# Sliding-block attention layers scored in 64x64 blocks, and unread matmuls also in the banks of a unit's tail

## The chip, the cores and the metric

The kernel runs on one core of one Trainium2 chip. A core has a matrix engine (TensorE, PE in the profile, with its weight loads as PEld), a vector engine (VectorE, DVE), a scalar engine that does the exps (ScalarE, ACT), a general engine (GpSimd, POOL) that here sets constants and issues some transfers, and a queue engine (SyncE, SP) that issues the others. Matmuls write to PSUM, eight banks of 512 fp32 columns in each of 128 partitions. The metric is the device time of one execution in microseconds.

## The reference, cut to what matters

Four layers alternate between kind A, a sliding-block attention, and kind B, a full one. Both have 2048 positions, 640 features, and 32 heads of 20.

```python
def attention(x, wqkv, wo, windowed):
    qkv = (x @ wqkv).reshape(B, S, 3, H, Dh).transpose(2, 0, 3, 1, 4)
    q, k, v = qkv[0], qkv[1], qkv[2]
    scores = jnp.einsum("bhqd,bhkd->bhqk", q, k) * (Dh ** -0.5)
    if windowed:                       # kind A, W = 256
        idx = jnp.arange(S)
        mask = (idx[:, None] - idx[None, :] >= 0) & (idx[:, None] - idx[None, :] < W)
        scores = jnp.where(mask[None, None], scores, -1e9)
    p = softmax(scores)
    o = jnp.einsum("bhqk,bhkd->bhqd", p, v)
    return o.transpose(0, 2, 1, 3).reshape(B, S, D) @ wo

x = x + attention(layernorm(x), A_wqkv, A_wo, True)
x = x + attention(layernorm(x), B_wqkv, B_wo, False)
x = x + attention(layernorm(x), A_wqkv, A_wo, True)
x = x + attention(layernorm(x), B_wqkv, B_wo, False)
```

In kind A a position sees itself and the 255 before it, so three 128-wide blocks of keys at most meet a 128-wide block of queries, and two of these three are cut by a diagonal.

## The kernel before

**Units and banks.** The work of attention is cut into units: one layer, one chunk of 512 queries (c, four of them) and one group of four heads (g, eight of them). The heads of a group lie in four strips of 32 partitions, so that a score matmul uses 32 rows of PE and four heads use four different strips. Scores are transposed: keys lie on the 128 PSUM partitions, queries on the columns. A *bank* is one PSUM bank of scores of one head. A full layer has 16 banks a head and unit, one for each block of 128 keys. A sliding-block layer has three banks a head and unit (`window_banks`): the six blocks of keys that a chunk of 512 queries can see are packed two into a bank, each over the query blocks that see it, so that a bank's 512 columns are filled: 128 + 384, 256 + 256 and 384 + 128. That is 1536 columns a head and chunk; the first chunk has only 512, 384 and 256. Each of these banks is multiplied after its exp by one of three patterns of zeros and ones (`masks`).

**Tiles and the main loop.** The banks of all units stand in one list, which is cut into *tiles* of three banks (in the early stretch three and two in turn). One turn of the main loop, a tick, does this for one tile: the score matmuls (L1222) into PSUM banks 0 to 2 or 3 to 5, in two rounds, first the first block of each bank and then the second; the exps (L1253), one ACT instruction for each run of banks with the same first column, into the tile `pt`; then other work that is let in by a credit (`pump`); then the value matmuls (L1289) of a group of four heads whose exps lie two or three ticks back, into bank 7; then the masking of the tile before (L1325, DVE). The order in which the instructions are written is the order in which they run on each engine.

**The other work.** Projections (`project`, L353, and `t_v`, L444), output projections (`t_out`, L530), layer norms (`t_ln`) and the *tail* of each unit (`t_tail`: column sums, their reciprocal, its spreading over the strips, and the product, in steps with waits of two ticks between them) are generators in a list `todo`, sorted by when they are needed. They take the PSUM banks that the tiles leave free, through `take_m` and `drop_m`: bank 6, and in the early stretch bank 5 too. `evac` copies a result out of PSUM, on ACT before the first unit of layer 1 and on DVE afterwards (`state["act"]`). Results for later layers are staged in `st` (pool `stp`, four tiles) and written to DRAM by POOL.

**The unread matmuls.** A clock is granted to PE at full or at half rate. `keep_clock` (L613) counts the PE work of a tick in `state["heat"]`, in units of one 512-column matmul, and while that is less than one for each bank (less a `surplus` carried over from the tick before), first lets in other work and then writes matmuls of the identity whose results nobody reads, into a free bank; if no bank is free it returns. It acts from the first unit of layer 1 (`woven`) to the end of layer 3's first chunk. In the tail of the very last unit `fill` (L981) does the same.

**The order of units.** Layer 0's units come first; layer 1's first chunk is mixed in as soon as its keys are there. Layer 2's units are mixed into layer 1's chunks 1 to 3 and the first chunk of layer 3. The rest of layer 3 stands alone.

## Time and profile before

| | |
|---|---|
| median of 4 runs | 2369.64 us (2365.09 to 2378.36) |
| the profiled execution's own time | 2370.41 us |
| its span, first to last instruction | 2368.7 us |
| mean granted clock of PE | 0.809 |
| exps of 1536 columns (L1253) | 1366, mean 1560 ns |
| exps of 1024 columns | 194, mean 1075 ns |
| unread matmuls (L613) | 549, 195.2 us busy |
| masks (L1325) | 403, 239.2 us busy |
| casts of projections to `st` on ACT (L302) / DVE (L304) | 23 / 127 |

By shape, the scores of the sliding-block layers are 512 matmuls of 384 columns (84.1 us busy), 448 of 256 (50.5 us) and 448 of 128 (53.0 us); their value matmuls are 512 of 384 (46.8 us), 448 of 256 (26.2 us) and 448 of 128 (28.1 us).

How to read the profile: it is one execution, its engines side by side. "Busy" is the time in which an engine runs at least one instruction, "idle before" the time it stood still in front of the instructions of a group, with what ended the wait. The chain is followed back from the last instruction to whatever released each step. Matmuls overlap, so the mean length of one says little of how many run in a microsecond; the distances of their starts do.

### The profile page before, as it was taken

The numbers are of one execution on the slowest core, as the hardware profiler recorded it, in microseconds if no ns is written. First come the engines' busy times: TensorE is split into PE (matmuls) and PEld (weight loads), VectorE is DVE, ScalarE is ACT, GpSimd is POOL, SyncE is SP. The second block draws the span as 40 slices with busy tenths as digits, with TensorE's granted clock in tenths as the row PEclk, the third lists the DMA queues.
The fourth block names the chain that finished last, engine by engine and source line by source line (L and its number), as shares of the span: only waits on it lengthen the run. The fifth ranks groups of instructions, "written<-read, shape, count | busy, mean of one in ns | idle before, by whom it ended". The sixth has DMA issues, their size and how long they took to land.

```text
span 2368.7 us, 40024 instructions
## 1 busy us (share of the span) xinstructions
PE 2030.5 (86%) x15554; PEld 708.9 (30%) x15554; DVE 1458.8 (62%) x2724; ACT 2184.9 (92%) x1753; POOL 142.9 (6%) x295
## 2 busy tenths in 40 slices
PE   8888999878888888888888888888878888888887
PEld 3433333323322332223322333232322222222222
DVE  7677775426646666656666544352577777777772
ACT  7778889898999998999899999999999999999997
POOL 3111110100000001000010011001000000000000
PEclk9999999997988998979997999889655565556556
DMA  6232422322300223102331034022111010001100
GB/s 183 72 96 80 109 64 58 83 62 64 82 19 27 57 68 93 37 14 54 75 93 32 3 86 118 29 42 73 51 34 37 26 38 26 26 26 38 38 14 12
DMA packets 173678, 132.53 MB, mean 56 GB/s; under 512 B 115760, under 2 KB 156080, under 8 KB 173488
## 3 DMA queue, kind: packets, MB, share of 16 engines
q1 hardware_dynamic: 163872, 101.39, 17.3%
q0 software_dynamic: 9616, 28.59, 3.5%
q8 instruction: 122, 2.00, 0.4%
q14 instruction: 68, 0.56, 0.1%
HBM read 98.70 MB, written 27.79 MB: 53 GB/s over the span
## 4 chain that ended last, share of the span: by engine, by line
ACT 36%; PE 31%; issue 16%; DVE 13%; DMA 2%; SPq 1%; POOL 0%; ACTq 0%; DVEq 0%; POOLq 0%
ACT pt L1253 35%; PE ps L1222 8%; PE ps L353 6%; PE ps L1289 5%; PE ps L530 4%; DVE pt L1325 3%; PE ps L444 3%; PE ps L613 2%; DMA wqk<-in_B_wqkv_dram 1%; DVE on L1020 1%; DVE st L304 1%; ACT ka L1253 1%; DVE oT L810 1%; DVE raw_o L858 1%; PE ps L1016 1%
## 5 line engine op out<-in xcount | busy, mean ns | idle before, releaser
L1253 ACT ACTIVATE pt<-ps 128x1536 bf16<-128x1536 f32 (+2 forms) x1641 | 2107.2, 1461 | 139.4 <-PE ps L1222 127.5
L1222 PE MATMUL ps<-qt,kt 32*128 32x512 bf16 x4008 | 671.2, 477 | 204.0 <-ACT pt L1253 173.4
L1289 PE MATMUL ps<-pt,vt 128*21 128x512 bf16 x3860 | 488.3, 478 | 1.0 <-DVE raw_o L796 0.7
L1222 PEld LDWEIGHTS <-kt 32*128 32x128 bf16 x4008 | 190.8, 94 | 650.8 <-issue 631.1
L1325 DVE TENSOR_TENSOR pt<-pt,masks 128x1024 bf16<-128x1024 bf16 (+5 forms) x403 | 239.2, 627 | 134.8 <-ACT pt L1253 134.2
L353 PE MATMUL ps<-xnT,wqk 128*128 128x512 bf16 x830 | 225.5, 397 | 25.5 <-DMA wqk<-in_B_wqkv_dram 10.8
L1289 PEld LDWEIGHTS <-vt 128*21 128x21 bf16 x3960 | 100.6, 91 | 335.6 <-issue 328.1
L613 PE MATMUL ps<-masks,ident 128*128 128x512 bf16 x549 | 195.2, 430 | 5.4 <-DVE rT L1008 2.0
L304 DVE CAST st<-ps 128x512 bf16<-128x512 f32 x127 | 87.8, 691 | 168.8 <-PE ps L353 168.3
L530 PE MATMUL ps<-wop,on 128*128 128x320 bf16 x976 | 170.7, 319 | 7.5 <-DVE on L1020 3.3
L1222 PE MATMUL ps<-qa,ka 32*128 32x384 bf16 (+2 forms) x1408 | 118.5, 278 | 35.6 <-ACT pt L1253 29.3
L858 DVE TENSOR_SCALAR xnT<-ps 128x512 int32<-128x512 f32 x88 | 60.8, 691 | 106.8 <-PE ps L851 104.2
L1020 DVE TENSOR_TENSOR on<-oT,ps 128x512 bf16<-128x512 bf16 x128 | 87.4, 683 | 60.9 <-PE ps L1016 60.5
L810 DVE CAST oT<-ps 128x512 bf16<-128x512 f32 x112 | 76.8, 686 | 72.4 <-PE ps L1289 46.7
L539 DVE TENSOR_TENSOR x_sb<-x_sb,ps 128x320 bf16<-128x320 bf16 x120 | 57.9, 482 | 101.7 <-PE ps L530 101.7
L444 PE MATMUL ps<-wv,xnT 128*128 128x320 bf16 x640 | 112.3, 309 | 7.5 <-DVE va L304 1.5
L530 PEld LDWEIGHTS <-on 128*128 128x128 bf16 x976 | 91.4, 102 | 75.4 <-issue 40.0
L353 PEld LDWEIGHTS <-wqk 128*128 128x128 bf16 x830 | 72.5, 99 | 125.9 <-issue 54.9
L1289 PE MATMUL ps<-pt,va 128*21 128x384 bf16 (+2 forms) x1408 | 80.4, 291 | 3.0 <-DVE pt L1325 1.8
L1222 PEld LDWEIGHTS <-ka 32*128 32x128 bf16 x1408 | 44.6, 92 | 104.9 <-issue 95.6
L444 PEld LDWEIGHTS <-xnT 128*128 128x128 bf16 x640 | 56.7, 99 | 50.4 <-issue 31.2
L1016 PE MATMUL ps<-rT,spread 32*128 32x128 bf16 x512 | 60.7, 250 | 5.3 <-DVE vs L304 2.1
(105 smaller groups left out, 1590.7 us busy)
## 6 DMA issues: line engine op xcount, KB each, us to landing
vt<-v_d SPq DMA_DIRECT2D x48, 336.0 KB
kt<-k_d SPq DMA_DIRECT2D x192, 80.0 KB
wqk<-in_B_wqkv_dram SPq DMA_DIRECT2D x80, 160.0 KB
wqk<-in_A_wqkv_dram SPq DMA_DIRECT2D x70, 160.0 KB
k_d<-st POOLq DMA_DIRECT2D x75, 128.0 KB, 2.2
q_d<-st POOLq DMA_DIRECT2D x75, 128.0 KB, 2.1
qt<-q_d SPq DMA_DIRECT2D x384, 20.0 KB
v_d<-vs POOLq DMA_DIRECT2D x16, 336.0 KB, 3.6
```

What stands on the lines that cost most here:

```text
L304: nc.vector.tensor_copy(out=out_, in_=in_)
L353: nc.tensor.matmul(pq, lhsT=wt[:, dc, :], rhs=xt[:, dc, :], start=(dc == 0), stop=(dc == KD - 1),)
L444: nc.tensor.matmul(pv, lhsT=xt[:, dc, i * P : (i + 1) * P], rhs=wv_sb[l % 2][:, dc, h * HD : (h + 1) * HD], start=(dc == 0), stop=(dc == K ...
L530: nc.tensor.matmul(yp, lhsT=on[:, g, qb * P : (qb + 1) * P], rhs=wop[:, g, i * HD : (i + 1) * HD], start=(g == g0), stop=(g == G - 1),)
L613: nc.tensor.matmul(ps[:, b, :], lhsT=ident[:], rhs=masks[:, 0, :], start=True, stop=True)
L810: nc.vector.tensor_copy(out=oT[:], in_=op)
L858: V.tensor_scalar(out=xi.bitcast(I32)[:, i * C : (i + 1) * C], in0=side["psum"], scalar1=SCALE * LOG2E * E23, scalar2=127.0 * E23, op0=ALU ...
L1020: nc.vector.tensor_tensor(out=on[:, g, :], in0=oT[:], in1=zb, op=ALU.mult)
L1222: nc.tensor.matmul(sp[:, i, col * P : (col + qn) * P], lhsT=u.k(kc, j), rhs=u.q(j, q0, qn), start=True, stop=True,)
L1253: nc.scalar.activation(out=pt[:, i:k, b0 * P :], in_=sp[:, i:k, b0 * P :], func=ACT.Exp, scale=SCALE,)
L1289: nc.tensor.matmul(op[32 * j : 32 * j + VW, q0 * P : (q0 + qn) * P], lhsT=u.v(kc, j), rhs=pg[:, i, col * P : (col + qn) * P], start=(first ...
L1325: nc.vector.tensor_tensor(out=pt_[:, i:k, b0 * P :], in0=pt_[:, i:k, b0 * P :], in1=mv_, op=ALU.mult,)
```

## The change

**Sliding-block scores.** The keys of a chunk are cut into blocks of 64 instead of 128. A score matmul has 64 keys (`half` 0 or 1 of a 128-wide block) as weights and writes the lower or the upper 64 PSUM partitions, over just those 64-wide query blocks that see its keys. A head and unit still has three banks: two *masked* windows of 512 columns (448 in the first chunk), each with three low and three high matmuls, and one bank of *pairs* of 256 columns (128 in the first chunk) that needs no mask. In all that is 1280 columns a head and chunk, 1024 in the first. The score loop now writes, for each bank of a tile, a low and a high matmul, and goes round until the longest list is done. If a tile holds any sliding-block bank, its full banks are scored in halves too.

**Exps.** A run of banks with the same first and last column is one instruction; before, only the first column counted, and it reached to the bank's end.

**Masks and values.** In two of a window's eight 64-wide columns the low and the high partitions hold different blocks of keys for different queries. The high half of these is multiplied into a separate small tile `phi` (a new pool of four), and the two stretches of three columns that hold diagonals and these high halves are multiplied in place, by `tri`, four 64-wide patterns in place of `masks`. The value matmuls read `phi` for those columns and `pt` for the others. `stp` has three tiles instead of four.

**Unread matmuls.** `keep_clock` keeps a `carry` of up to 3 over the ticks; the heat of the scores is no longer added; the least heat is the tile's width in columns/512, divided by 3, times 1.76 (times 1.0 in front of `woven`, where nothing was asked for until now). A tail that takes a bank writes an unread matmul into it first (`warm_bank`) when the heat is below the least and no other work can be let in. The unread matmul reads the identity four times over instead of `masks`. In a tile of sliding-block banks the credit for other work is scaled by its width/2.5.

By the order of instructions, the number of exps goes from 1641 to 1699, the masks from 403 to 524 instructions, the score matmuls of the sliding-block layers from 1408 to 3712, their value matmuls from 1408 to 2752, the unread matmuls from 558 to 658, and the casts to `st` on ACT from 23 to 14. POOL and SP issue the same transfers as before.

```diff
+B = 64
+    phip = pool("phip", 4)
-    stp = pool("stp", 4)
+    stp = pool("stp", 3)
-    masks = big.tile([P, 3, C], BF16, name="masks", tag="masks")
+    tri = big.tile([P, 4, B], BF16, name="tri", tag="tri")
+    idents = ident[:].unsqueeze(1).to_broadcast((P, 4, P))
...
+    def cool():
+        return state["heat"] + state["carry"] < state["least"]
+    def unread(b):
+        nc.tensor.matmul(
+            ps[:, b, :].rearrange("p (a b) -> p a b", a=4), lhsT=ident[:], rhs=idents,
+            start=True, stop=True,
+        )
+        state["heat"] += 1.0
+    def warm_bank(b):
+        if cool() and (
+            state["credit"] <= 0.0 or all(task.wake > state["tick"] for task in todo)
+        ):
+            unread(b)
-    def keep_clock(least):
-        while state["heat"] < least:
+    def keep_clock():
+        while cool():
             t = choose(False)
             if t is not None and state["credit"] > -0.5:
                 state["credit"] -= advance(t)
                 continue
             b = min(mfree, key=mfree.get)
             if mfree[b][0] > state["tick"]:
-                return
+                break
+            unread(b)
+        spare = state["heat"] + state["carry"] - state["least"]
+        state["carry"] = min(max(spare, 0.0), 3.0)
+        state["heat"] = 0.0
...
+    def windows(c):
+        found = []
+        for o in range(2):
+            k, q = 4 * c + o, 2 * o
+            low = [(k, q, 5, 1), (k + 2, q + 4, 2, 6)]
+            high = [(k, q + 1, 5, 2), (k + 2, q + 5, 1, 7)]
+            values = [
+                (k, q, 5, 1, False), (k + 2, q + 4, 2, 6, False), (k, q + 5, 1, 6, True),
             ]
+            if c > 0:
+                low.append((k - 2, q, 1, 0))
+                high.insert(1, (k - 2, q, 2, 0))
+                values = [(k - 2, q, 1, 0, False), *values, (k - 2, q + 1, 1, 1, True)]
+            else:
+                high[0] = (k, q, 6, 1)
+            found.append(((0 if c > 0 else B, C), True, low, high, values))
+        pairs = [(4 * c + 2, 6, 2, 0)] + [(4 * c - 1, 0, 2, 2)] * (c > 0)
+        found.append(((0, 2 * B * len(pairs)), False, pairs, pairs, [(*p, False) for p in pairs]))
...
         mb = yield from take_m()
+        warm_bank(mb)
         zp = ps[:, mb, 0:16]
...
+        def mask(pt, hi, i, k, first):
+            v = pt[:, i:k, :]
...
+            nc.vector.tensor_tensor(
+                out=hi["t"][:, i:k, int(first) :, :], in0=w[:, :, 6 if first else 1 : 7 : 5, :],
+                in1=tri[:, 3:4, :].unsqueeze(1).to_broadcast((P, n, 2 - first, B)), op=ALU.mult,
+            )
...
+            x = bass.AP(v.tensor, v.offset, [(ps_, pn), (ss, n), (5 * B, 2), (1, 3 * B)])
+            m = tri[:, 0:3, :].rearrange("p b e -> p (b e)")
+            nc.vector.tensor_tensor(
+                out=x, in0=x,
+                in1=m.unsqueeze(1).unsqueeze(1).to_broadcast((P, n, 2, 3 * B)), op=ALU.mult,
+            )
...
-                for n in range(2):
-                    for i, (u, j, m, b0, subs, first, last, end) in enumerate(cur):
-                        for kc, q0, qn, col in subs[n : n + 1]:
+                for n in range(0, max(len(x) for x in jobs), 2):
+                    for i, x in enumerate(jobs):
+                        for half, lhsT, rhs, col in x[n : n + 2]:
+                            rows = slice(0, P) if half is None else slice(B * half, B * half + B)
                             nc.tensor.matmul(
-                                sp[:, i, col * P : (col + qn) * P],
-                                lhsT=u.k(kc, j), rhs=u.q(j, q0, qn), start=True, stop=True,
+                                sp[rows, i, col : col + rhs.shape[1]],
+                                lhsT=lhsT, rhs=rhs, start=True, stop=True,
                             )
...
+                width = sum(b[3][1] - b[3][0] for b in cur) / C
+                warmth = 1.76 if state["unit"] >= woven else 1.0
+                state["least"] = warmth * width / 3 if state["unit"] < index[3, 1, 0, None] else 0.0
                 load_ahead()
                 r = rate(t)
+                if cur[0][2] is not None and cur[-1][2] is not None:
+                    r *= width / 2.5
                 pump(r, r + 0.1)
-                state["heat"] += 0.414 * n_b
-                if woven <= state["unit"] < index[3, 1, 0, None]:
-                    keep_clock(1.0 * n_b - surplus)
-                surplus = min(max(surplus + state["heat"] - 1.0 * n_b, 0.0), 1.0 * n_b)
-                state["heat"] = 0.0
+                keep_clock()
```

## The prediction

> **What bounds the kernel now.** I read the granted clock first, then the busy shares, the chain, the stretches between the sliding-block stages, the groups by shape, and last the order of time inside single tiles. The page:
>
> ```profile
> span 2368.7 us, 40024 instructions
> PE 2030.5 (86%) x15554; PEld 708.9 (30%) x15554; DVE 1458.8 (62%) x2724; ACT 2184.9 (92%) x1753; POOL 142.9 (6%) x295
> PEclk9999999997988998979997999889655565556556
> ACT 36%; PE 31%; issue 16%; DVE 13%; DMA 2%; SPq 1%; POOL 0%; ACTq 0%; DVEq 0%; POOLq 0%
> ```
>
> ACT, which does the exps, is full for 92% of the span, but the chain that ended last lies as much on PE as on ACT. So I cut the span where the program changes: first sliding-block score (15.6), first full score (167.4), last score of layer 0 (408.5), first of layer 2 (630.0), last of layer 2 (1553.4).
>
> ```profile
> core 0: us, PE busy (x) PEld busy (x) DVE busy (x) ACT busy (x) POOL busy (x), PEclk, DMA share, GB/s
> 15.60:167.40 151.80, 132.59 (x1193) 60.78 (x1195) 104.89 (x267) 119.53 (x169) 27.39 (x57) 0.94 0.37 97
> 167.40:408.50 241.10, 219.09 (x2000) 88.06 (x2001) 165.38 (x355) 208.40 (x181) 30.22 (x57) 0.96 0.31 81
> 408.50:630.00 221.50, 189.81 (x1414) 70.25 (x1411) 101.86 (x208) 203.09 (x159) 16.48 (x30) 0.91 0.29 72
> 630.00:1553.40 923.40, 796.76 (x6476) 285.82 (x6473) 542.53 (x1040) 869.54 (x673) 49.51 (x99) 0.90 0.21 54
> 1553.40:2368.70 815.30, 681.29 (x4429) 199.32 (x4424) 534.03 (x828) 777.62 (x567) 8.85 (x16) 0.61 0.12 34
> ```
>
> Layer 0 (15.6 to 408.5, 392.9 us) is led by PE: 351.7 us busy against ACT's 327.9. Layer 2's stretch is led by ACT: 869.5 of 923.4. Behind 1553.4 only half the clock is granted and ACT still has 95%. The groups the change touches, in the view by line and shape:
>
> ```profile
> L1253 ACT ACTIVATE pt<-ps 128x1536 bf16<-128x1536 f32 x1366 | 1892.7, 1560 | 124.3 <-PE ps L1222 114.3 <-ACT pt L1253 1.9 <-issue 1.7
> L613 PE MATMUL ps<-masks,ident 128*128 128x512 bf16 x549 | 195.2, 430 | 5.4 <-DVE rT L1008 2.0 <-DVE rz L995 1.5 <-DVE on L1020 1.0
> L1325 DVE TENSOR_TENSOR pt<-pt,masks 128x1024 bf16<-128x1024 bf16 x132 | 89.3, 683 | 32.0 <-ACT pt L1253 31.8
> L1325 DVE TENSOR_TENSOR pt<-pt,masks 128x1536 bf16<-128x1536 bf16 x86 | 81.3, 951 | 48.8 <-ACT pt L1253 48.5
> L1325 DVE TENSOR_TENSOR pt<-pt,masks 128x512 bf16<-128x512 bf16 x134 | 54.8, 418 | 52.9 <-ACT pt L1253 52.9
> ```
>
> In order of time, ACT alone, then PE (start, length, last the idle before):
>
> ```profile
> 1108.25 9.52 ACT L1253 ACTIVATE pt<-ps 128x1536 bf16<-128x1536 f32 x7 [0.28 <-PE ps L1222]
> ...
> 1148.89 1.45 ACT L1253 ACTIVATE pt<-ps 128x1536 bf16<-128x1536 f32 x1 [0.79 <-PE ps L1222]
> ```
>
> ```profile
> 160.32 0.11 PEld L1289 LDWEIGHTS <-va 128*21 128x21 bf16 x8 [0.42 <-issue]
> 160.32 0.40 PE L1289 MATMUL ps<-pt,va 128*21 128x128 bf16 x8
> ...
> 160.65 0.12 PEld L1222 LDWEIGHTS <-ka 32*128 32x128 bf16 x6 [0.22 <-issue]
> 160.66 0.39 PE L1222 MATMUL ps<-qa,ka 32*128 32x128 bf16 x6
> ```
>
> Seven full exps take 9.52 us, one alone 1.45: (9.52 - 1.45)/6 = 1.35 from start to start. The medians of starts without idle are 1331 ns for 1536 columns, 904 for 1024, 691 for 768, 478 for 512, 264 for 256: 0.833 ns a column and 51 ns an instruction. On PE, four value matmuls on four column strips of the same 128 rows start within 11 ns; the next four follow 63 ns later, for 128 columns that stream in 53 (512 columns take 215 at the full clock: five of L353 in 1.19 us). Each change of tile shape costs about 94 ns between the last column streamed (160.557) and the next weight load (160.651).
>
> **ACT.** A head and chunk falls from 1536 exp columns to 1280, in the first chunk from 1152 to 1024. Per layer: 24 units x 4 heads x 256 + 8 x 4 x 128 = 28,672 columns x 0.833 = 23.9 us. Exps of unlike column ranges can't be one instruction, so there are 1699 of them for 1641: 58 x 51 ns = 3.0 us, half a layer. Each layer saves 22.4 us of ACT. The projections' credit in a sliding-block tile is now scaled by width/2.5, so fewer projections come before ACT hands evacuation to DVE: 9 st, 8 va and 3 xnT move, 9 x 0.48 + 8 x 0.31 + 3 x 0.57 = 8.5 us off ACT and 9 x 0.69 + 11 x 0.49 = 11.6 us onto DVE, all in layer 0.
>
> **PE scores.** Columns that all matmuls of these layers stream: 368,640 before, in 128-wide weights; 622,592 after, in 64-wide ones. If the two halves of a head run beside each other, that is 311,296: at three heads a tile (57,344/3) x 0.42 ns = 8 us less, 4 a layer. No row here shows 32-row strips and column strips split at once: value matmuls show column strips together, scores (six loads within 22 ns, above) row strips. If halves follow each other, (622,592 - 368,640)/3 x 0.42 = +35 us; if in-order issue then also holds back the next head, a tile's three heads take four half-streams where one is due, and 311,296/3 x 0.42 = 43 us become some 170, +120 over now's 51. 58 full banks that share a tile with sliding ones are scored in halves too, which costs nothing in the first case. I take the lower end, by the rows nearest to it, and keep the rest as a rival. Score rounds rise from 565 to 761; a round shows 7 to 14 ns over its columns (63 or 67 less 53): 2 to 3 us.
>
> The Trainium skill speaks against this: TensorEngine Tiling (Array Packing), section Restrictions and Gotchas, says that column tiling excludes Fast Weight Load, and TensorE: Matmul & The Clock Gate, section LDWEIGHTS, gives columns/1.2 ns for a plain load, 53 ns for 64 columns. As an estimate from that page, 761 rounds with an open 53 ns would be 40 us of PE where the rows give 3; in this trace loads of 21 columns (90 ns) and of 128 (92 to 102) hardly differ and hide behind the running matmul.
>
> **PE values.** The same 368,640 columns in 688 rounds for 352: 336 x 7 to 36 ns (a 64-column round streams in 27, and none is shown; the upper end is the 128-column round's 63) = 2 to 12 us; I take 4.
>
> **Unread matmuls and tile shapes.** 658 for 558. By the instruction order, L613's go 57 to 25 in 167.4 to 408.5, 65 to 89 in 408.5 to 630, 392 to 474 in layer 2's stretch, and the last stretch has 26 more. 100 x 0.215 = 21.5 us of PE at the full clock. Those in a tail's bank hold up the tail's next step by 0.2 us, which has two tiles of time. Changes of tile shape go from 3684 to 3853: 169 x 0.094 = 16 us, 108 of them in layer 2's stretch. Against that stands the clock: from 600 to 1640 half of it was granted for 205 us, and ACT was idle 13.7% of those against 3.8% of the rest. Holding it throughout is worth at most 9.9% x 205 = 20 us there.
>
> **DVE.** Masks: 403 instructions, 239.2 us. After: 233 into phi and 291 in place. The rows give 0.146 us + 0.53 ns a column (256: 0.282, 512: 0.418, 1024: 0.685): 64 + 142 = 207 us, 33 less; pairs need none. A masked three-bank tile is 0.35 + 0.75 = 1.10 where 0.95 was, still under one exp. No row has the new strided form; at the rate of the fp32 product (L879, 1.22 us per 1024 columns against 0.685) it would add 90 us to an engine that is 59 to 69% busy there. I take the bf16 rate. The cover of the extra mask instruction is the window's value lag of three tiles; without it, PE would stand still 0.15 us at each of the 233 mask groups, 34 us.
>
> **Queues and pools.** SP and POOL issue the same transfers. Three staging tiles for four: none of the 150 casts into st in this trace began before the write three earlier had landed, so it costs nothing; without that cover a cast waits some 2.2 us. phi has four tiles against three in flight.
>
> **The sum.** Layer 0: PE leads; -4 scores, +2 values, -32 x 0.215 = -7 unread, +1 shapes: -8. ACT's 31 counts only where the chain is on exps, I take 2. So -10 (0 to -31). 408.5 to 630: +5 unread, +2 shapes, against 41 us of half clock: 0 (-4 to +5). Layer 2: ACT -22; PE -4 + 2 + 18 + 10 = +26, a third of it on the path, because PE has 14% free: +8; a third of the clock's 20 back: -7. So -21 (0 to -42). Last stretch: 26 unread at its head, +8 on PE, a quarter shown: +2. Sum -29. The profiled run took 2370.4 us (span 2368.7), 0.8 over the median of the runs, so 2341.
>
> **Rivals.**
> A. The halves do not run together. For it: no row shows it, and two halves read the same 32 rows. Against: four value matmuls read the same 128 rows together. Price: 43 to 127 of PE over my sum, half of it a layer. Layer 0, led by PE, pays all its half; layer 2 pays what exceeds its free 14%, about half. In the middle, 85 x (0.5 + 0.25) = +64: 2405. It decides from +41 on the path, where the 29 are gone and 12 more.
> B. PE gives it back. The 48 us of new unread matmuls, shapes and rounds meet shorter exp tiles (a tile of pairs is 0.69 us where 1.33 stood), so ACT waits for scores; for it, 47.3 us of ACT idle before exps end on a score in layer 2's stretch now. Then layer 2 gains 0 to 5 and layer 0 5: 2363.
> C. All of ACT's gain shows and the clock holds: 22 + 20 in layer 2, 31 in layer 0, and 4 between: -77, of which PE's 352 us in layer 0 allows about half: 2308.
>
> **Chances.** Forecast 0.54 (own range 2320 to 2358), A 0.14, B 0.18, C 0.14. Range 2303 to 2398: all of the forecast, B, C's most and half of A, 0.86 or so, no wider because A's upper half is left out. Half a per cent, 12 us, is what a measurement tells from no change. Faster: forecast, C, a little of B: 0.70. Same: most of B, 0.12. Slower: A and B's tail, 0.18.
>
> **What would show it.** Right: exps of 1280 columns a head at 51 ns + 0.833 a column; six 64-wide loads and matmuls of a round within some 22 ns; layer 2's stretch near 902 us with ACT still over 93%; the last stretch unchanged within 3 us. Wrong: a second half that starts only when the first has streamed (A); ACT idle behind scores above 54 us in layer 2's stretch (B); in-place masks near 1.3 us for 1152 columns; clock lower than 0.90 there although more matmuls are unread.

## The result: no change, because layer 0 gave back what the rest gained

Over 35 runs the changed kernel took 2371.8 us at the median (2361.49 to 2384.75), beside 2371.6 for the kernel before on the same chips. The ratio is 0.9998, with a 95% interval of 0.9987 to 1.001. The forecast was 2341, with a range of 2303 to 2398: the time lies in the range, but of the 29 us forecast nothing shows. The profiled execution took 2368.87 us. Executions of one kernel lie about 1% apart (1.4% in e1 and 2.1% in e7 below) and go with the mean granted clock (e1: 2341.62 us at 0.846, 2374.20 at 0.827), so the verdicts stand on medians and intervals, and a stretch of a single profile says less (how much less is measured below).

The page of the changed kernel:

```profile
span 2367.2 us, 47904 instructions
...
PE 2033.2 (86%) x19360; PEld 774.5 (33%) x19360; DVE 1431.2 (60%) x2865; ACT 2135.7 (90%) x1791; POOL 140.2 (6%) x291
...
PEclk9978999999899899999998899999855565556556
...
ACT 36%; PE 32%; issue 16%; DVE 12%; DMA 2%; SPq 1%; POOL 1%; ACTq 0%; DVEq 0%; POOLq 0%
```

ACT is busy for 49 us less, PE for 3 more, the mean granted clock is 0.832 for 0.809, and the span is 1.5 us shorter. The saved work did turn up, as idle time of ACT. Where it did is shown by the stretches, cut at the same events as before: first sliding-block score, first full score, last score of layer 0, first of layer 2, last of layer 2, end. (Columns: start and end, length, then busy time of PE, PEld, DVE, ACT and POOL with instructions in brackets, granted clock, share and rate of the DMA.)

```profile
14.90:152.40 137.50, 119.93 (x1875) 64.22 (x1875) 94.29 (x308) 100.58 (x152) 21.39 (x44) 0.90 0.33 91
152.40:427.30 274.90, 242.56 (x3130) 112.97 (x3117) 168.71 (x394) 200.25 (x200) 35.39 (x69) 0.91 0.30 81
427.30:646.20 218.90, 188.43 (x1468) 73.33 (x1465) 101.75 (x208) 201.51 (x160) 16.50 (x30) 0.97 0.30 72
646.20:1555.70 909.50, 795.02 (x8388) 316.99 (x8385) 522.73 (x1099) 850.42 (x707) 49.49 (x99) 0.95 0.22 55
1555.70:2367.20 811.50, 676.95 (x4484) 202.57 (x4483) 533.60 (x829) 776.07 (x569) 8.86 (x16) 0.63 0.13 34
```

| stretch | before | after | difference | forecast |
|---|---|---|---|---|
| layer 0 (first two rows) | 392.9 | 412.4 | +19.5 | -10 |
| to the first score of layer 2 | 221.5 | 218.9 | -2.6 | 0 |
| layer 2 | 923.4 | 909.5 | -13.9 | -21 |
| the rest | 815.3 | 811.5 | -3.8 | +2 |

The head in front of these is 0.7 shorter. The miss lies in layer 0. Its ACT is busy for 301 us where it was 328, and idle for 112 where it was 65. Its PE had half the clock for 79 us where it was 34. The view of waits for its second half, before and after (waiting engine and line, what it waited for, us in all, times, longest):

```profile
ACT pt L1253 <- PE ps L1222: 29.9, 39, 3.5
```

```profile
ACT pt L1349 <- PE ps L1318: 65.2, 58, 7.1
...
PEld L1318 <- DMA ka<-k_d: 12.8, 7, 5.8
PE ps L1318 <- DMA ka<-k_d: 10.2, 4, 5.5
```

The exps wait for scores, and some of the scores wait for keys that are still on their way from DRAM. (One stall is listed at the weight load, PEld, and again at its matmul, PE, so the 12.8 and the 10.2 us are largely the same time.) Before, waits of scores for `qa` and `ka` came to 0.3 us in that stretch. The chain of waits shows it in order of time (four of the pieces between 166 and 206 us: start, length, what):

```profile
169.29 1.98 DMA q_d<-st
...
172.40 1.69 DMA ka<-k_d
...
192.51 3.57 DMA q_d<-st
...
200.20 1.63 DMA ka<-k_d
```

Before each of these pairs stand a projection (L352) and its cast to `st`; behind each stand scores (L1318). The store in these pieces is one of queries and the load behind it one of keys. Layer 0 has become a line of projection, store, load, score: queries and keys are made so late that their way through DRAM is no longer covered.

The exps, the masks and the halves of the scores came out about as they were priced from rows (the masks 203 us for 207). In the view by line and shape (busy us, mean ns of one, idle time before it and who ended it):

```profile
L1349 ACT ACTIVATE pt<-ps 128x1536 bf16<-128x1536 f32 x1277 | 1765.3, 1574 | 135.8 <-PE ps L1318 121.3 <-ACT pt L1349 6.0 <-issue 2.1
...
L608 PE MATMUL ps<-ident 128*128 128x512 bf16 x649 | 228.6, 402 | 21.3 <-DVE rT L1067 9.7 <-DVE on L1080 4.2 <-DVE rz L1053 1.9
...
L1263 DVE TENSOR_TENSOR pt<-pt,tri 128x1152 bf16<-128x1152 bf16 x77 | 58.4, 758 | 2.8
...
L1248 DVE TENSOR_TENSOR phi<-pt,tri 128x384 bf16<-128x384 bf16 x77 | 26.9, 349 | 27.1 <-ACT pt L1349 27.1
```

The strided in-place mask of 1152 columns takes 758 ns, where the contiguous ones of that width in the kernel before took 747:

```profile
L1325 DVE TENSOR_TENSOR pt<-pt,masks 128x1152 bf16<-128x1152 bf16 x9 | 6.7, 747 | 1.0 <-ACT pt L1253 1.0
```

And the halves run side by side, in the timeline of the changed kernel (start, length of the group, instructions, idle before):

```profile
1506.72 0.42 PE L1318 MATMUL ps<-qa,ka 32*64 32x320 bf16 x18 [0.39 <-ACT pt L1349]
1506.73 0.28 PEld L1318 LDWEIGHTS <-ka 32*64 32x64 bf16 x17 [0.36 <-issue]
```

18 matmuls of 32x64 tiles of the array are through in 0.42 us. The six of the first round start 3 to 4 ns apart, and the next round starts 135 ns after it, in which 320 columns stream once (320 x 0.42 ns = 134).

### The profile page after: what moved, and what is told of

Its sections match the earlier page's. It is cut to its first block, busy times and chain, and to the rows that moved or that the text cites. A ratio compares the mean times of both kernels' runs of the same rounds, so it can differ in the third digit from the quotient of the medians.

```text
span 2367.2 us, 47904 instructions
## 1 busy us (share of the span) xinstructions
PE 2033.2 (86%) x19360; PEld 774.5 (33%) x19360; DVE 1431.2 (60%) x2865; ACT 2135.7 (90%) x1791; POOL 140.2 (6%) x291
## 4 chain that ended last, share of the span: by engine, by line
ACT 36%; PE 32%; issue 16%; DVE 12%; DMA 2%; SPq 1%; POOL 1%; ACTq 0%; DVEq 0%; POOLq 0%
ACT pt L1349 35%; PE ps L1318 8%; PE ps L352 6%; PE ps L1386 5%; PE ps L529 5%; PE ps L443 3%; PE ps L608 2%; DVE pt L1263 2%; DVE on L1080 1%; DVE st L303 1%; DVE oT L866 1%; ACT ka L1349 1%; DVE phi L1248 1%; DMA wqk<-in_B_wqkv_dram 1%; PE ps L1076 1%
## 5 line engine op out<-in xcount | busy, mean ns | idle before, releaser
L1349 ACT ACTIVATE pt<-ps 128x1536 bf16<-128x1536 f32 (+5 forms) x1699 | 2066.3, 1397 | 191.1 <-PE ps L1318 167.3
L1318 PE MATMUL ps<-qt,kt 32*128 32x512 bf16 (+1 forms) x4066 | 651.9, 461 | 186.8 <-ACT pt L1349 154.4
L1318 PEld LDWEIGHTS <-kt 32*128 32x128 bf16 (+1 forms) x4066 | 190.9, 94 | 599.0 <-issue 571.3
L352 PE MATMUL ps<-xnT,wqk 128*128 128x512 bf16 x830 | 230.6, 404 | 23.7 <-DMA wqk<-in_B_wqkv_dram 5.4
L608 PE MATMUL ps<-ident 128*128 128x512 bf16 x649 | 228.6, 402 | 21.3 <-DVE rT L1067 9.7
L1318 PE MATMUL ps<-qa,ka 32*64 32x128 bf16 (+3 forms) x3712 | 121.7, 246 | 36.9 <-ACT pt L1349 23.1
L1248 DVE TENSOR_TENSOR phi<-pt,tri 128x128 bf16<-128x128 bf16 (+4 forms) x233 | 64.7, 278 | 125.4 <-ACT pt L1349 124.4
L352 PEld LDWEIGHTS <-wqk 128*128 128x128 bf16 x830 | 72.9, 100 | 123.2 <-issue 55.0
L1263 DVE TENSOR_TENSOR pt<-pt,tri 128x1152 bf16<-128x1152 bf16 (+2 forms) x175 | 104.4, 597 | 6.4
L1318 PEld LDWEIGHTS <-ka 32*64 32x64 bf16 x3712 | 75.7, 105 | 93.0 <-issue 63.7
L608 PEld LDWEIGHTS <-ident 128*128 128x128 bf16 x649 | 49.1, 97 | 103.3 <-issue 96.9
L1386 PE MATMUL ps<-pt,va 128*21 128x128 bf16 (+2 forms) x1856 | 76.6, 249 | 6.6 <-DVE pt L1263 4.9
```

The lines of the kernel that those rows point to most:

```text
L352: nc.tensor.matmul(pq, lhsT=wt[:, dc, :], rhs=xt[:, dc, :], start=(dc == 0), stop=(dc == KD - 1),)
L608: nc.tensor.matmul(ps[:, b, :].rearrange("p (a b) -> p a b", a=4), lhsT=ident[:], rhs=idents, start=True, stop=True,)
L1248: nc.vector.tensor_tensor(out=hi["t"][:, i:k, int(first) :, :], in0=w[:, :, 6 if first else 1 : 7 : 5, :], in1=tri[:, 3:4, :].unsqueeze(1) ...
L1263: nc.vector.tensor_tensor(out=x, in0=x, in1=m.unsqueeze(1).unsqueeze(1).to_broadcast((P, n, 2, 3 * B)), op=ALU.mult,)
L1318: nc.tensor.matmul(sp[rows, i, col : col + rhs.shape[1]], lhsT=lhsT, rhs=rhs, start=True, stop=True,)
L1349: nc.scalar.activation(out=pt[:, i:k, a:e], in_=sp[:, i:k, a:e], func=ACT.Exp, scale=SCALE,)
```

## The experiments

Numbers of a stretch are from one profiled execution; ratios are against the kernel before in the same batch, with 95% intervals. "Half clock" is the time in which half of PE's clock was granted.

How far a single profile can be trusted is seen in e1, e6 and e7. e6 and e7 differ from e1 in layer 0 alone, and in layer 2's stretch all three run the same 8382 weight loads in the same order. The stretch took 907.1, 918.0 and 901.8 us, with 92, 137 and 75 us of half clock:

```profile
626.20:1533.30 907.10, 792.26 (x8384) 319.70 (x8382) 523.21 (x1099) 848.43 (x707) 49.36 (x99) 0.95 0.22 55
638.70:1556.70 918.00, 804.83 (x8353) 321.44 (x8382) 523.10 (x1099) 850.19 (x707) 49.32 (x98) 0.93 0.21 54
663.70:1565.50 901.80, 781.96 (x8353) 319.25 (x8382) 522.93 (x1099) 847.53 (x706) 49.39 (x99) 0.96 0.22 55
```

So a difference of layer 2's stretch between two single profiles is not shown by them alone while it is under some 16 us, and that holds for the -13.9 above; it needs the medians or a second pair. ACT's busy time is steadier (847.5 to 850.2).

### Layer 0: is it the scaled credit?

**e1** is the changed kernel without the scaling.

```diff
-                if cur[0][2] is not None and cur[-1][2] is not None:
-                    r *= width / 2.5
```

> The changed kernel without the line that scales the credit for other work by width/2.5. Theory D (deferred work): in layer 0 the smaller credit puts the projections off until score matmuls wait for keys and queries that have yet to be stored and loaded; without it the last layer-0 score comes at 385 to 400 us (427 in the changed kernel, 408 before), ACT's idle time in 152 to 427 falls from 75 to 45 us or less, and the whole kernel takes 2335 to 2350 us. Theory H (half clock): layer 0 is longer because its unread matmuls fell from 57 to 25; then this run keeps the last layer-0 score at 420 to 430 and the whole at 2365 to 2375. Theory S (smaller score matmuls and the split masks cost it): the same as H here.

**e2** keeps it in layer 2 alone.

```diff
-                if cur[0][2] is not None and cur[-1][2] is not None:
+                if cur[0][0].l == 2 and cur[0][2] is not None and cur[-1][2] is not None:
```

> The scaling of the credit kept in layer 2 alone. Theory D: layer 0 as in the run without any scaling (last score at 385 to 400), layer 2's stretch as in the changed kernel (909 us), whole 2335 to 2350. If the scaling helps layer 2, this is 3 to 10 us faster than the run without any. H and S: 2365 to 2375.

**e8** is the kernel before with nothing but the scaling in layer 0, by the widths that the new tiles have.

```diff
+                if cur[0][2] is not None and cur[0][0].l == 0 and cur[-1][0].windowed:
+                    wide_, part_ = (1.0, 0.5) if cur[0][0].c else (0.875, 0.25)
+                    third = 2 if cur[0][0].c else 1
+                    r *= sum(part_ if b[2] == third else wide_ for b in cur) / 2.5
```

> The kernel before, whole, with only the credit scaling of layer 0, by the widths that its tiles would have in the changed kernel. Theory D: layer 0 ends 12 to 22 us later than 408.5 although scores, exps, masks and unread matmuls are all as before, with score matmuls that wait for the loads of keys; whole 2380 to 2392. If the scaling hurts only beside the changed scores: layer 0 within 4 us of 408.5, whole 2366 to 2376.

e1: 2362.07 us, ratio 0.9951 (0.9922 to 0.998); e2: 2360.66, 0.9954 (0.9933 to 0.9976). Layer 0 is back at 393.7 and 397.3 us. (e1's profiled execution, 2345.02 us, was one of its fastest.) e8: 2379.45, 1.0052 (1.0025 to 1.008), layer 0 at 402.6, +9.7 on before. Its waits, in the stretch of its profile that answers to those shown above:

```profile
ACT pt L1253 <- PE ps L1222: 45.8, 46, 5.2
...
PE ps L1222 <- DMA qa<-q_d: 7.9, 4, 3.6
```

With the old scores, the old masks and the old exps, the scaling alone brings the scores that wait for a load. The same holds over all profiles: in the four with scaling in layer 0 (changed kernel, e3, e8, e13) matmuls of scores wait 10.2, 9.9, 8.1 and 10.0 us for such loads, and in e1, e2 and the kernel before not at all. So the scaling as cause is shown by taking it away and by adding it alone. It costs 9 to 10 us at the median (2371.8 less 2362.1; 2379.5 less the 2370.8 of the kernel before in that batch). e2, which keeps it in layer 2, is as fast as e1, so the cost lies in layer 0. The sizes fell short of what was expected: e1 and e2 were put at 2335 to 2350, with the last score of layer 0 at 385 to 400 us, and it came at 408.6 and 412.8; e8's layer 0 was put at 12 to 22 us longer.

The other candidate was the clock, since the scaling also took unread matmuls out of layer 0 (25 for 57) and its half-clock time rose. It is not the main part. e6 (below) has no scaling and no unread matmul in layer 0, and 72 us of half clock there, nearly the 79 of the changed kernel; its layer 0 took 398.1 us, 4.4 more than e1's and 14 less than the changed kernel's. e3 (below) has the scaling and the old rule for unread matmuls; its layer 0 took 422.5. So of the 19 us between the profiles of e1 and the changed kernel, the waits for loads are some 10 and the clock perhaps 4; the rest is not accounted for.

### Layer 0: does the shorter ACT bring anything there?

Without the scaling layer 0 still gained nothing (393.7 for 392.9), though ACT had 19 us less to do. The four experiments here all start from e1.

**e5** does the pairs' exps over all 512 columns from the second chunk on; 256 of them are never read.

```diff
+                    wide = C if e == C // 2 else e
-                        out=pt[:, i:k, a:e], in_=sp[:, i:k, a:e], func=ACT.Exp, scale=SCALE,
+                        out=pt[:, i:k, a:wide], in_=sp[:, i:k, a:wide], func=ACT.Exp, scale=SCALE,
```

> The kernel without the credit scaling, with its exps of pairs run over all 512 columns behind the first chunk (256 of them old scores whose exps nobody reads): ACT does as much as in the kernel before, PE, DVE and the unread matmuls do what they did. This prices the saved exp columns alone: 2 x 24,576 columns x 0.833 ns = 41 us of ACT. Theory P (PE paces layer 0, and part of layer 2): layer 0's end moves by 3 us or less from 408.6, layer 2's stretch grows from 907 to 914 to 924, whole 8 to 18 us over the run without scaling. Theory A (ACT paces both and something else ate the gain): layer 0's end moves by 15 to 20 us and layer 2's stretch by 20, whole 30 to 40 us more.

**e10** is e5 with the wide columns counted in `width` too, since e5 lowered the least heat in relation to the tile's time.

```diff
-                width = sum(b[3][1] - b[3][0] for b in cur) / C
+                width = sum((C if b[3][1] == C // 2 else b[3][1]) - b[3][0] for b in cur) / C
```

> The run with pairs' exps over 512 columns once more, with those 512 counted in the least heat too, so that a tile that lasts as long as before also asks for as many unread matmuls as before. In the first of these two runs layer 2's stretch had 184 us at half clock against 92, so it priced columns and clock together. If the columns alone are worth what ACT's busy time says: half-clock time there back at 75 to 110 us, ACT 20 us busier than without, layer 2's stretch 917 to 927, whole 2370 to 2378. If new scores and masks cost nothing of themselves, it equals the kernel before with the new unread rule (917 and 2363) within 4 us; if they cost PE or DVE time on the path, it lies 5 to 15 us over that.

**e6** has no unread matmuls in layer 0.

```diff
+                if state["unit"] <= index[0, NC - 1, G - 1, None]:
+                    state["least"] = 0.0
```

> The kernel without the credit scaling, and with no unread matmul up to the last unit of layer 0 (51 fewer in 167 to 409). If PE's work is what paces layer 0: 51 x 0.215 = 11 us less PE, layer 0 ends 5 to 11 us sooner than 408.6. If the clock is worth more than the work: more time at half clock than 38 us in layer 0, and its end moves out by 3 to 15 us. If PE waits for something else: within 3 us.

**e7** has more credit in layer 0.

```diff
-                return 1.2
+                return 1.6
...
-            return min(1.1 * r, 1.0 if u.l == 0 else 0.9)
+            return min((1.4 if u.l == 0 else 1.1) * r, 1.3 if u.l == 0 else 0.9)
```

> The kernel without the credit scaling, with a third more credit for other work in layer 0 (1.6 for 1.2, and a higher cap while layer-0 units run). Theory D carried on: if projections still come late, layer 0 ends 5 to 15 us sooner. Theory P: PE does the same work in another order, and the end stays at 405 to 412; ACT's idle time moves from the later part of layer 0 to the earlier.

e5's layer 0, to be held against the same two stretches of e1:

```profile
15.80:169.60 153.80, 132.34 (x1953) 71.18 (x1970) 97.20 (x313) 116.34 (x172) 26.34 (x56) 0.93 0.36 96
169.60:410.60 241.00, 215.63 (x3026) 103.98 (x3048) 154.51 (x369) 209.82 (x200) 30.32 (x58) 0.98 0.31 82
```

```profile
14.90:166.90 152.00, 132.76 (x1971) 70.66 (x1975) 96.88 (x313) 110.53 (x172) 26.32 (x56) 0.94 0.36 99
166.90:408.60 241.70, 221.29 (x3049) 104.67 (x3048) 154.53 (x369) 198.00 (x199) 30.29 (x58) 0.96 0.31 82
```

ACT is busy for 17.6 us more in e5 (326.2 for 308.5) and layer 0 is 1.1 us longer; e10, with ACT as busy (326.9), took 403.4 us there. The pair e1 and e5 alone would be thin, but the other profiles agree with it: in the kernels with the new exps and no scaling in layer 0 (e1, e2, e11, e12, e14, e17) it took 393.7 to 398.4 us, and with the old exps (before, e4, e15, e18) 388.9 to 393.7. Some 19 us less of ACT never made layer 0 shorter, so ACT does not pace it; the idle time before its exps takes up what it saves. Over the whole, e5 took 2378.19 us (1.0035; 1.0012 to 1.0059) and e10 2373.71 (1.0014; 0.9996 to 1.0032): in layer 2 the wide exps, 20 to 22 us more of ACT, went with 943.7 and 928.6 us for e1's 907.1, and e5's excess over e10 goes with 184 us of half clock for 113. e10's layer 0 stood 8.6 us above e5's with the same exps and a higher least heat; no run tells whether that is more than the spread of single profiles.

What does pace layer 0 these runs didn't settle. e6 removed its 51 unread matmuls, some 11 us of PE at the full clock, and layer 0 became 398.1, with 72 us of half clock for 38; the whole took 2366.68 (0.9978; 0.9958 to 0.9998), an interval that overlaps e1's. Less PE work and less clock came together, so this doesn't isolate PE's work. e7 let projections in sooner, which was expected to help or to change nothing, and was worse: 2405.42 us (1.0113; 1.0078 to 1.0148). Its profiled execution, 2375.78 us, was the fastest of its ten and has layer 0 at 432.6; why more credit costs so much was not looked into. The credit as it stood in the kernel before lies between two worse ones.

### The unread matmuls and the clock

"Least heat" is the amount of PE work below which a tick is filled up with unread matmuls. **e4** puts the new rule for them (least heat, carry, tail banks) into the kernel before and leaves the scores as they were; `width` is there that of the old exps.

```diff
-        while state["heat"] < least:
+        while cool():
...
+        spare = state["heat"] + state["carry"] - state["least"]
+        state["carry"] = min(max(spare, 0.0), 3.0)
+        state["heat"] = 0.0
...
+        warm_bank(mb)
...
+                width = sum(C - b[3] * P for b in cur) / C
+                warmth = 1.76 if state["unit"] >= woven else 1.0
+                state["least"] = warmth * width / 3 if state["unit"] < index[3, 1, 0, None] else 0.0
```

> The kernel before with the new rule for unread matmuls alone. D: layer 0 unchanged within 3 us (last score at 406 to 412); layer 2's stretch loses 5 to 15 us from its 923 because less of it is at half clock; whole 2355 to 2366. H: layer 0 ends 10 to 20 us later, at 418 to 428, whole 2370 to 2385.

**e3** is the changed kernel with the old rule.

```diff
-        if cool() and (
+        if False and (
...
-        while cool():
+        while state["heat"] < least:
...
-                keep_clock()
+                state["heat"] += 0.414 * n_b
+                if woven <= state["unit"] < index[3, 1, 0, None]:
+                    keep_clock(1.0 * n_b - surplus)
+                surplus = min(max(surplus + state["heat"] - 1.0 * n_b, 0.0), 1.0 * n_b)
+                state["heat"] = 0.0
```

> The changed scores, exps and masks with the kernel before's rule for unread matmuls (heat of the scores counted, no unread matmul in a tail's bank, least heat by the number of banks). Theory H: layer 0 gets its unread matmuls back and ends 10 to 20 us sooner, at 407 to 417. Theory D: layer 0 ends where the changed kernel's does, 420 to 432. Both: layer 2's stretch has more time at half clock (96 us in the changed kernel, 188 before) and is 5 to 15 us longer than 909. Whole: 2375 to 2390 by D, 2360 to 2370 by H.

**e12** is e1 without the unread matmuls in the tails' banks.

```diff
-        if cool() and (
+        if False and (
```

> The kernel without the credit scaling and without the unread matmuls in a tail's banks; the rest of the new unread rule stays. If the tail's banks are what holds the clock: half-clock time in layer 2's stretch goes from 92 to 150 us or more, the whole to 2368 to 2376. If the carry and the new counting do it: half-clock time stays under 120 us and the whole within 4 us of 2362.

Layer 2's stretch of e4, and of e12:

```profile
625.10:1541.80 916.70, 791.06 (x6582) 292.47 (x6579) 543.25 (x1040) 867.41 (x673) 49.36 (x99) 0.96 0.21 54
```

```profile
635.60:1548.50 912.90, 792.99 (x8281) 311.17 (x8278) 522.75 (x1100) 849.22 (x707) 49.94 (x99) 0.90 0.21 55
```

| | median | ratio | layer 2 | half clock there | unread there |
|---|---|---|---|---|---|
| before | 2371.6 | 1 | 923.4 | 188 | 392 |
| e4, rule alone | 2363.20 | 0.9976 (0.9949 to 1.0003) | 916.7 | 75 | 498 |
| e3, all but the rule (credit scaled) | 2388.19 | 1.008 (1.0052 to 1.0108) | 916.6 | 195 | 393 |
| e12 | 2373.93 | 1.0023 (1.0006 to 1.004) | 912.9 | 188 | 367 |
| e1 | 2362.07 | 0.9951 (0.9922 to 0.998) | 907.1 | 92 | 471 |

That the new rule pays is shown by two pairs whose intervals don't meet. e12, without the unread matmuls in the tails' banks, is back at 188 us of half clock in layer 2 and loses 12 us at the median against e1. e3, the changed kernel without the rule, is 16 us slower than the changed kernel and slower than the kernel before. Against the kernel before, e4's median is 6.4 us lower, but its interval reaches 1, and the 6.7 us in layer 2's stretch are within the spread of single profiles. They go with 106 more unread matmuls there (some 23 us of PE at 0.215 us each) and a granted clock of 0.96 for 0.90.

### The least heat by width

The changed kernel asks for less heat where a tile has fewer exp columns. In these it is asked for by banks: **e11** on e1, without the credit's scaling;

```diff
-                width = sum(b[3][1] - b[3][0] for b in cur) / C
+                width = n_b
```

> The kernel without the credit scaling, with the least heat by the number of banks and not by their width: more unread matmuls beside the short tiles of pairs (some 40 more in layer 2's stretch). If idle time behind short exps is PE at half clock: half-clock time there falls from 92 us to 60 or less, the stretch from 907 to 895 to 903, whole 2350 to 2358. If PE's own work is what the short tiles don't cover: the stretch grows by 2 to 8 us, whole 2364 to 2370.

**e13** on the changed kernel, with the scaling, and **e16** on e2, with the scaling in layer 2 alone, both by this edit:

```diff
-                state["least"] = warmth * width / 3 if state["unit"] < index[3, 1, 0, None] else 0.0
+                state["least"] = warmth * n_b / 3 if state["unit"] < index[3, 1, 0, None] else 0.0
```

> The changed kernel whole, credit scaling too, with the least heat alone taken by the number of banks. If the two scalings act on their own (17 us from the heat, 10 from the credit): layer 0 still ends at 420 to 432, layer 2's stretch falls from 909 to 897 to 903, whole 2351 to 2358. If the heat's gain needs the unscaled credit: whole 2364 to 2372.

> The credit scaling in layer 2 alone, least heat by banks. If the scaled credit helps short tiles of layer 2: stretch 3 to 8 us under 899.5, whole 2336 to 2342. If it does nothing, as in the pair of runs with the least heat by width (2362.1 without, 2360.7 with): 2342 to 2348.

| ratio (layer 2's stretch, us) | least heat by width | by banks |
|---|---|---|
| credit scaled | after: 0.9998 (909.5) | e13: 1.0003 (906.4) |
| scaled in layer 2 alone | e2: 0.9954 (906.7) | e16: 0.9931 |
| not scaled | e1: 0.9951 (907.1) | e11: 0.9894 (899.5) |

The two don't add. With the credit scaled, asking by banks brings nothing at the median; without it, 17 us at the median (2344.65, 0.9869 to 0.9919), and the intervals of e1 and e11 don't meet. The profiles can't show where: e1's was one of its fastest, so that the two profiled executions took the same time (2345.02 and 2344.91 us). e16's profiled execution took 2387.67 us, 1.6% over its median, so no stretch of it stands here. e16 took 2350.86 (0.9907 to 0.9955), between them, and its interval overlaps e11's. So the scaling in layer 2 is free by width and perhaps not by banks; that stays open, and so does why the two don't add.

### The new scores at an equal clock

The factor of the least heat is raised from 1.76 to 2.0 (**e14**, **e15**) and to 2.3 (**e17**, **e18**): in e14 and e17 with the new scores, from e11, in e15 and e18 with the old ones, from e4.

```diff
-                warmth = 1.76 if state["unit"] >= woven else 1.0
+                warmth = 2.0 if state["unit"] >= woven else 1.0
```

> The kernel with neither scaling (2344.65), and 2.0 for 1.76 in the least heat: some 70 more unread matmuls. If more half-clock time can still be bought back: layer 2's stretch has under 40 us of it (55 now) and falls to 888 to 896, whole 2330 to 2341. If PE's load now costs more than the clock gives: stretch 900 to 910, whole 2345 to 2356.

> The kernel before with the new unread rule (2363.2) and 2.0 for 1.76: more unread matmuls without new scores. This tells whether the 17 us of the run with the least heat by banks belong to the new scores' short tiles or would come from more unread matmuls anyhow. If from the short tiles: here 2358 to 2368, layer 2's stretch 910 to 920. If from more unread matmuls in general: 2345 to 2352, stretch 898 to 905.

> Neither scaling, and 2.3 in the least heat (2.0 gave 2334.7, 34 us of half clock in layer 2's stretch of 891). If the clock still pays: half-clock time under 25 us, stretch 882 to 889, whole 2322 to 2332. If PE's own work is now what ACT waits for: stretch 892 to 905, whole 2336 to 2350.

> The kernel before with the new unread rule and 2.3 (2.0 gave 2343.2). Beside the run with the new scores at 2.3 it prices the new scores where the clock is nearly always whole: ACT is 19 us busier in layer 2's stretch here. If ACT sets that stretch once the clock holds, the difference there grows from 11 us (at 2.0) to 15 to 20 and the whole is 2340 to 2350; if the short tiles go on giving half of it back as idle time, the difference stays at 8 to 12 us.

Layer 2's stretch of e14, and of e15:

```profile
626.90:1518.00 891.10, 786.53 (x8463) 316.02 (x8457) 521.83 (x1099) 846.79 (x706) 49.53 (x99) 0.98 0.22 56
```

```profile
629.80:1531.70 901.90, 784.45 (x6620) 291.23 (x6617) 542.20 (x1040) 865.50 (x673) 49.65 (x99) 0.98 0.22 55
```

With the same clock and the same 34 us of half clock, ACT is 18.7 us less busy and 7.9 more idle, and the stretch 10.8 shorter.

e10 beside e4 shows the other side. e10 has the new scores and masks, but its wide exps keep ACT as busy in layer 2 as the old ones did in e4 (868.1 and 867.4 us), and both ask for unread matmuls by the same rule:

```profile
638.10:1566.80 928.70, 812.18 (x8410) 323.50 (x8404) 524.80 (x1100) 868.12 (x707) 50.00 (x99) 0.94 0.21 54
```

e10's stretch is 12 us longer than e4's, nearly all of it idle time of ACT (60.6 us for 49.3), with 113 us of half clock for 75, and the whole is 10.5 us slower at the median (2373.71 and 2363.20). So the new scores, masks and values seem to cost some 10 us of their own, beside what the shorter exps save. It is not shown firmly: the two intervals overlap a little (e4's reaches 1.0003, e10's begins at 0.9996).

| factor | new scores: median, ratio | old scores: median, ratio | layer 2, new and old | layer 0, new and old |
|---|---|---|---|---|
| 1.76 | e11: 2344.65, 0.9894 | e4: 2363.20, 0.9976 | 899.5, 916.7 | 398.4, 393.7 |
| 2.0 | e14: 2334.71, 0.9865 (0.9842 to 0.9888) | e15: 2343.15, 0.9883 (0.9856 to 0.991) | 891.1, 901.9 | 394.0, 393.3 |
| 2.3 | e17: 2336.31, 0.9858 (0.9827 to 0.9889) | e18: 2335.54, 0.9869 (0.9832 to 0.9906) | 891.8, 903.7 | 394.4, 388.9 |

In the profiles layer 2 is 10.8 and 11.9 us shorter with the new scores. But e14's and e17's profiled executions lie 5.4 and 6.8 us under their medians and those of e15 and e18 at theirs, so part of this may be spread. Over the whole the intervals overlap at 2.0 and at 2.3; the medians differ by 8.4 us at 2.0 and by 0.8 us, the other way, at 2.3. In the profiles, e18 takes 5.6 us less in layer 0 and 1.0 less up to layer 2; how much of that is spread, four runs each don't tell. Raising the factor brings more with the old scores (2363.20 to 2335.54) than with the new ones (2344.65 to 2336.31). Four of these, e14, e15, e17 and e18, beat the kernel before by 1.2 to 1.4%, and none of them measurably another. So at 2.3 nothing measurable is left of the new scores in the whole time: e18, with the old ones, is as fast as any. Of what was expected, e11, e15 and e18 came out 2 to 5 us faster than their ranges, e16 3 us slower, and e5's layer 2 20 us longer.

## Why the prediction was wrong, step by step

**The step that failed.** "The projections' credit in a sliding-block tile is now scaled by width/2.5, so fewer projections come before ACT hands evacuation to DVE" was priced as 8.5 us off ACT and 11.6 onto DVE. The count of moved evacuations was right (on ACT in layer 0 `st` 23 to 14, `va` 24 to 16, `xnT` 12 to 9); their lateness was not priced at all. A projection that comes later makes its store, its load and the scores behind them later, and in layer 0 these are due at once. The sum had nothing for it. In its place the runs showed matmuls of scores that stand 8 to 10 us for loads wherever layer 0's credit is scaled; e1, e2 and e8 measured some 10 us at the median, and the profiles of the changed kernel and e1 differ by 19 in layer 0. The warning stood in the step's own words: it moved work, and work that is moved has somebody who waits for it.

**Layer 0's -10 was not there either.** PE was to be 8 us less busy. In the changed kernel it was busy for 362.5 us there, with more half clock, where it had been 351.7; without the scaling (e1) for 354.1. Scores: -4 forecast, 62.8 to 62.4 us measured. Values: +2 (half of the 4 taken, within 2 to 12 for both layers), measured 39.1 us before and up to 51.3 in e1, 36.8 from `pt` and 14.5 from `phi` as far as these don't overlap: at most 12 us more for one layer, twice its share of the range's upper end. Unread matmuls: 32 fewer forecast and found in the changed kernel, but only 6 fewer in e1 (51 for 57). That only 2 of ACT's 31 us were taken as a gain was right, and even 2 was too much by the profiles listed above.

**Layer 2's terms came near.** Forecast was -21: ACT -22, PE +8, clock -7. The view by line in layer 2's stretch, before and after:

```profile
L1253 ACT ACTIVATE pt<-ps 128x1536 bf16<-128x1536 f32 (+5 forms) x673 | 871.1, 1458 | 53.9 <-PE ps L1222 48.4 <-ACT pt L1253 1.9 <-PE ps L1006 0.8
```

```profile
L1349 ACT ACTIVATE pt<-ps 128x1536 bf16<-128x1536 f32 (+6 forms) x707 | 851.8, 1350 | 59.1 <-PE ps L1318 53.3 <-ACT pt L1349 1.8 <-issue 1.0
```

In the rows of the stretches ACT is busy for 19.1 us less and idle for 5.2 more, which is the measured -13.9. So ACT's term was 3 too large, and PE's and the clock's together are +5 where +1 was forecast. Taken apart, at an equal clock (e14 against e15, e17 against e18) ACT is 18.7 and 19.0 us less busy and 7.9 and 7.0 more idle; against the rule for unread matmuls alone e4's stretch shows -6.7, its extra PE work included. These singles lie within the spread of one profile, and that they agree with the terms is in part luck. One step the prediction named nowhere with a price: its least heat follows the width. A sliding-block tile with fewer exp columns still has nearly the same PE work in it, and asking for less there cost 17 us at the median without the scaled credit (e1 against e11, 92 us of half clock in layer 2 for 55). With the scaled credit, as in the changed kernel, asking by banks brought nothing (e13), so how much of the changed kernel's time this step explains stays open.

**The last stretch and the one between.** +2 and 0 forecast, -3.8 and -2.6 measured. The 26 more unread matmuls at the head of the last stretch, charged for a quarter of their length, didn't show as a cost: its half clock fell from 643 to 606 us, for which the sum had credited nothing. In all profiles with unread matmuls in the tails this stretch took 808.5 to 812.3 us, in those without (before, e3, e8, e12) 814.1 to 815.7.

**The rivals.** A needed halves that follow one another; 18 matmuls in 0.42 us refute it. For A the prediction had drawn on the Trainium skill: on TensorEngine Tiling (Array Packing), section Restrictions and Gotchas, for column tiling being without Fast Weight Load, and on TensorE: Matmul & The Clock Gate, section LDWEIGHTS, for the length of a load, from which it estimated 40 us of open weight loads. The trace doesn't show them; the loads lie beside running matmuls (0.28 of the 0.42 us above). B, "PE gives it back", with 2363, came nearest in time, but mostly by another mechanism: the loss was in layer 0 and its waits for loads. In layer 2 its mark, ACT idle behind scores above 54 us, was just missed (53.3, up from 48.4), and e10 beside e4 shows that some of what it describes does happen there. C wanted all of ACT's gain in layer 2 and more in layer 0; even e14, the fastest at the median, has 891.1 in layer 2 for C's 881, and nothing in layer 0.

## What to carry to other kernels

A parameter that paces background work is part of the path of whoever reads that work's result: when a change scales it, count the moved instructions, and then ask of each which transfer and which consumer it makes late. A saving on the busiest engine counts in the stretches that this engine paces, and an extra load on it (e5, e10) helps to tell which these are, as long as it doesn't change the clock with it. Where a meter that is meant for one engine is tied to another one's work, compare variants at the same granted clock before crediting the new work with anything. And two runs with the same instructions in a stretch tell how far that stretch moves by itself.

## What the runs showed of the hardware

- Matmuls that nobody reads held the clock over a wide range: in layer 2's stretch with the old scores, 392 by the old rule and 498, 536 and 665 by the new one went with 188, 75, 34 and 27 us of half clock, 923.4, 916.7, 901.9 and 903.7 us, and 2371.6, 2363.2, 2343.2 and 2335.5 us in the whole at the median.
- Half the clock remained in the last stretch of every kernel (0.60 to 0.63) although in the changed kernel PE was 83% busy there (677 of 811.5 us) and never idle for more than 1.38 us at a time. The Trainium skill, TensorE: Matmul & The Clock Gate, section "HAM oscillation — how this bites in real kernels", gives as the abstract rule that no idle gap of PE be over some 3.4 us; gaps below that did not keep the clock here. Its next section, "A second HAM failure mode: psum-queue depth-cycling", tells of a kernel in which short, frequent idling made the clock go back and forth; here it stayed at half for up to 198 us on end.
- ACT's idle share in half-clock time between 600 and 1640 us went from 13.7% to 26.3% while that time fell from 205 to 107 us, so ACT's idle time in it stayed at 28.0 us. It did not shrink with the half clock, as the prediction's price for the clock (9.9% of that time) had it.
- Tiles of the array with both rows and columns split (32x64) ran six at once (the 18 matmuls in 0.42 us above); the prediction had no row for it.
- A mask with a pattern of four dimensions, in place, in bf16 ran within 2% of contiguous ones (758 ns for 1152 columns, 747 contiguous).
